# VectorE's filter arithmetic placed instruction by instruction between the steps of the ELU layer

## The chip, the cores and the metric

The kernel runs on one core of a Trainium2 chip. The metric is the device time of one execution in microseconds (us); lower is better. All data are float32.

## The reference

A global filter layer is followed by a two-layer network with an ELU. The filter is a real Fourier transform along the sequence, a product with a complex filter, and the inverse transform:

```python
X = np.fft.rfft(x, axis=1)              # x: 8 x 3008 x 256
F = (filt_r + 1j * filt_i)[None, :, :]  # 1505 x 256
y = np.fft.irfft(X * F, n=3008, axis=1)
t = y.reshape(24064, 256)
h = t @ w_in                            # 256 x 2048
g = np.where(h > 0.0, h, np.exp(np.minimum(h, 0.0)) - 1.0)
out = g @ w_out                         # 2048 x 256
```

## The kernel before

**Two kinds of work, interleaved.** There are eight images. The filter of image b is computed while the ELU layer of image b-1 runs; the first image's filter and the preparation of the weights come ahead of everything. The order of all instructions is written out by hand.

**The ELU layer.** An image has six token blocks (m = 0..5), each with four slices of the hidden layer (q = 0..3). One (b, m, q) is called a *quad*; 192 of them run one after the other, 24 (`PER`) for each image. Tokens come 512 at a time (448 for m = 0), as two halves. Both matrix products are done on 2 x 2 blocks with seven products instead of eight (Strassen's scheme in Winograd's form), so a quad has seven *up* steps (`up_steps`: into the hidden layer, matmuls on line 629) and seven *down* steps (`down_steps`: out of the hidden layer, matmuls on line 711; those of the quad before). A step is four matmuls. The loop at the end of the kernel deals the steps out by strings such as `"UUDUDDU"` and then `"DUUDUDD"`; quads in `opens` have other strings.

The seven products yield four blocks of the hidden layer: b11, b12, b21, b22. ScalarE copies single products out of PSUM (L640); VectorE adds the others to them (`add`, L637): b11 in up step `s2`, b22 in `s7`, b21 in `s4`. The bank `phd` is filled in `s7`, read by VectorE for b22, and then filled further in `s4`. The ELU takes two ScalarE instructions (`elu_exp`, L646 and L647) and one on VectorE (`elu_max`, L651, the maximum). By program order VectorE does in a quad: b11's add; the b22 add and the maximum of b11 (`s7`); the maximum of b12 (`s3`); b21's add and the maximum of b22 (`s4`); and in the tail two differences (L687, L688), the maximum of b21, and two more differences (L690, L691). In `s3`, ScalarE's exponentials of b12 and b22 are issued ahead of the maximum of b12.

After four quads the down products are combined: ScalarE copies two banks (L717), VectorE adds two of them and the two other banks in `tail` of `down_steps`, two more sums in `c_unit` a quad later, the last two and the transposes in `o_unit` the quad after that (all L728; transposes L753); then the output is written.

**Places.** `at(quad, place, fn, ...)` puts other work into a quad: place 2 after the third step of the first string and place 3 after its fifth, place 0 between the strings, place 1 behind the quad and its tails. This holds for one image's filter, with s the quad of its first step for a group g of frequencies (s = 6, 10, 14, 18 from the image's start):

- quad s, place 1: `b_unit`, the short transforms (TensorE), copies and sums;
- s + 1, place 2: `re_mult`, four products (L455, L456); place 1: `re_sums`, four sums (L462, L464);
- s + 2, place 2: three of the four products of `im_mult` (L472), all four for g = 4; place 1: the rest of them and `im_join`, two sums (L477);
- s + 3, place 2: `im_sums`, two sums (L482); place 1: `bi_unit`, the inverse short transforms, and the writes to DRAM.

`x_unit` (L230, L231) makes sums and differences of the inputs at place 0. `n_sums` (L604, L606) makes the five sums that the up steps need of a token block; for m = 1 two of them stand at place 2 of quad 2 of an image's 24, and three at place 1 of the same quad. The filter's table is read by GpSimd's DMA queue (`f_read`, L366), the intermediate tensors go through DRAM by SyncE's.

PSUM has four banks for the up steps and the transforms (`banks`, first in, first out) and four for the down steps.

Of the kernel before, what the change touches and what calls it, by code (L numbers as in the profile page):

```python
# [11 lines left out]
FP32 = mybir.dt.float32  # L12
U32 = mybir.dt.uint32
AXT = mybir.ActivationFunctionType
ALU = mybir.AluOpType
# [26 lines left out]
def _make_tables():  # L42
# [81 lines left out]
    tn = np.ascontiguousarray(tn.transpose(2, 1, 0, 3, 4, 5)).reshape(P, H, 64)  # L124
    once = np.stack([np.eye(P), gf.reshape(P, P)], 1)
    return [t.astype(np.float32) for t in (ta, tc, tn, np.stack([gb, gr, gi], 1), tf, once, pairs, tw)]


def order(m):
# [5 lines left out]
def kernel(  # L135
# [310 lines left out]
            nc.vector.tensor_tensor(out=t[:, k + 1], in0=t[:, k + 1], in1=ps, op=ALU.subtract)  # L446
        banks.extend(pf[p][0] for p in (0, 3, 1, 2))

    def re_mult(b, g):
        t, f = rs[b, g], fall[:, 0:2]  # L450
        z = ss[b, g] = qp.tile([P, 4, 2, D], FP32, tag="z", name="zs")
        if g == 0:
            nc.scalar.activation(out=t[0:32, :, 0, :], in_=once_in[0:32], func=AXT.Copy)
        for c in range(2):
            nc.vector.tensor_tensor(out=z[:, 2 + c], in0=t[:, c], in1=f[:, :, 0, c, :], op=ALU.mult)  # L455
            nc.vector.scalar_tensor_tensor(out=z[:, c], in0=t[:, 2 + c], scalar=-1.0, in1=f[:, :, 1, c, :],  # L456
                                           op0=ALU.mult, op1=ALU.mult)

    def re_sums(b, g):
        z = ss[b, g]  # L460
        for c in range(2):
            nc.vector.tensor_tensor(out=z[:, 2 + c], in0=z[:, 2 + c], in1=z[:, c], op=ALU.add)  # L462
        for c, op in ((0, ALU.add), (1, ALU.subtract)):
            nc.vector.tensor_tensor(out=z[:, c], in0=z[:, 2], in1=z[:, 3], op=op)  # L464
        if g == 0:
            nc.gpsimd.tensor_copy(out=z[0:32, 0:2, 0, :], in_=z[0:32, 2:4, 0, :])

    def im_mult(b, g, *parts):
        t, f = rs[b, g], fall[:, 0:2]
        for c, h in parts:  # L470
            k = 2 * h + c
            nc.vector.tensor_tensor(out=t[:, k], in0=t[:, k], in1=f[:, :, 1 - h, c, :], op=ALU.mult)  # L472

    def im_join(b, g):
        t = rs[b, g]
        for c in range(2):
            nc.vector.tensor_tensor(out=t[:, c], in0=t[:, c], in1=t[:, 2 + c], op=ALU.add)  # L477

    def im_sums(b, g):
        t, z = rs.pop((b, g)), ss[b, g]  # L480
        for c, op in ((0, ALU.subtract), (1, ALU.add)):
            nc.vector.tensor_tensor(out=z[:, 2 + c], in0=t[:, 0], in1=t[:, 1], op=op)  # L482
        if g == 0:
            for c in range(2):
                nc.gpsimd.tensor_copy(out=z[0:32, 2 + c, 0, :], in_=t[0:32, 1 - c, 0, :])

# [127 lines left out]
    def up_steps(b, m, q):  # L614

        h = half(m)
        y = ys[b, m]
        g = {}
        for tag, names in G_TAGS:
            t = gp.tile([P, len(names), 2, 256], FP32, tag=tag, name=tag)  # L620
            g.update({n: t[:, i, :, 0:h] for i, n in enumerate(names)})
        held = {}

        def mm(n, key, start):
            if start:
                held[key] = bank("ph" + key)
            ps = held[key][1]
            for a in range(2):
                nc.tensor.matmul(ps[:, a, 0:h], w_in[q][:, COMBO[n], a, :], y[n],  # L629
                                 start=start and a == 0, stop=True, skip_group_check=True)  # L630
            return ps[:, :, 0:h]

        def done(key):
            banks.append(held.pop(key)[0])

        def add(o, i0, i1):
            nc.vector.tensor_tensor(out=g[o], in0=i0, in1=i1, op=ALU.add)  # L637

        def keep(o, i0):
            nc.scalar.activation(out=g[o], in_=i0, func=AXT.Copy)  # L640

        es = {}

        def elu_exp(n, src):
            e = es[n] = ep.tile([P, 2, 256], FP32, tag="e", name="e")[:, :, 0:h]
            nc.scalar.activation(out=e, in_=src, func=AXT.Relu, scale=-1.0)  # L646
            nc.scalar.activation(out=e, in_=e, func=AXT.Exp, scale=-1.0)  # L647

        def elu_max(n, src):

            nc.vector.scalar_tensor_tensor(out=g[n], in0=es[n], scalar=1.0, in1=src, op0=ALU.subtract, op1=ALU.max)  # L651


        def s1():
            keep("t1", mm(1, "s", True))

        def s2():
            add("b11", mm(2, "a", True), g["t1"])
            done("a")

        def s6():
            keep("t2", mm(6, "s", False))

        def s5():
            keep("t4", mm(5, "s", False))

        def s7():
            elu_exp("b11", g["b11"])
            add("b22", mm(7, "d", True), g["t4"])
            elu_max("b11", g["b11"])  # L670

        def s3():
            p = mm(3, "s", False)
            elu_exp("b12", p)
            elu_exp("b22", g["b22"])
            elu_max("b12", p)
            done("s")

        def s4():
            add("b21", mm(4, "d", False), g["t2"])  # L680
            done("d")
            elu_max("b22", g["b22"])

        def tail():
            elu_exp("b21", g["b21"])
            t1, b12, b22 = g["t1"], g["b12"], g["b22"]
            nc.vector.tensor_tensor(out=t1, in0=b12, in1=g["b11"], op=ALU.subtract)  # L687
            nc.vector.tensor_tensor(out=b12, in0=b22, in1=b12, op=ALU.subtract)  # L688
            elu_max("b21", g["b21"])
            nc.vector.tensor_tensor(out=g["t2"], in0=b22, in1=t1, op=ALU.subtract)  # L690
            nc.vector.tensor_tensor(out=g["t4"], in0=g["b21"], in1=g["t2"], op=ALU.subtract)  # L691
            g_of[b, m, q] = {1: g["b11"], 2: g["b21"], 3: b22, 4: g["t4"], 5: t1, 6: g["t2"], 7: b12}

        return (s1, s2, s6, s5, s7, s3, s4), tail


    PLACE = {1: (0, 0), 5: (0, 1), 3: (1, 0), 7: (1, 1), 2: (2, 0), 6: (2, 1), 4: (3, 0)}

    def down_steps(b, m, q):
# [19 lines left out]
        def tail():  # L719
            if q != 3:  # L720
                return
            p1, p5 = (k[0][:, u, 0:h] for u in range(2))
            p35, p7 = (k[1][:, u, 0:h] for u in range(2))
            c = kp.tile([P, 2, 512], FP32, tag="c", name="c")
            (c11, c12), (c21, c22) = ((c[:, i, 0:h], c[:, i, h:2 * h]) for i in range(2))

            def add(o, i0, i1):
                nc.vector.tensor_tensor(out=o, in0=i0, in1=i1, op=ALU.add)  # L728

            add(p35, p35, p5)  # L730
            add(c12, po[2][:, 1, 0:h], p1)
            add(c11, po[2][:, 0, 0:h], p1)
            rest = [(p7, p7, c12), (c21, po[3][:, 0, 0:h], p7), (c12, c12, p35), (c22, p7, p5)]
            cs_[b, m] = c, lambda i: [add(*r) for r in rest[i:i + 2]]

        return [(lambda n=n: step(n)) for n in DOWNS], tail

# [2 lines left out]


    def c_unit(b, m):
        cs_[b, m][1](0)

    def o_unit(b, m):
        c, join = cs_.pop((b, m))
        join(2)
        o = kp.tile([P, 2, 2, 256], FP32, tag="k", name="o").rearrange("p i u (j s) -> p (i u j) s", s=64).rearrange("p j (e s) -> p j e s", e=2)
        if last(b, m):
            return o_last(b, m, c, o.rearrange("p (k f j) e s -> p k f (j e s)", k=2, f=2))  # L750
# [135 lines left out]
    with tc.manual_schedule():  # L886
# [135 lines left out]
        def at(quad, place, fn, *a):  # L1022
            plan.setdefault((quad, place), []).append((fn, a))
# [16 lines left out]
        for b in range(B):  # L1040
            t = (b - 1) * PER
            if b > 0:
# [15 lines left out]
                for g in range(0, NG, 2):  # L1058
# [4 lines left out]
                        if g:  # L1063
                            at(s - 1, 0, z_read, b, k)
                    at(s, 1, b_unit, b, g)
                    at(s + 1, 2, re_mult, b, g)
                    at(s + 1, 1, re_sums, b, g)
                    parts = ((0, 0), (0, 1), (1, 0), (1, 1))
                    early = 4 if g == 4 else 3
                    at(s + 2, 2, im_mult, b, g, *parts[:early])  # L1070
                    at(s + 2, 1, im_mult, b, g, *parts[early:])
                    at(s + 2, 1, im_join, b, g)
                    at(s + 3, 2, im_sums, b, g)
                    at(s + 3, 1, bi_unit, b, g)
                    at(s + 3, 1, y_write, b, g)
            for m, (s, sums) in enumerate(((23, (((23, 0), 0, 1, 2), ((24, 2), 3, 4))), (25, (((26, 2), 0, 1), ((26, 1), 2, 3, 4))),
                                           (25, (((29, 0), 0, 1), ((29, 1), 2, 3, 4))), (32, (((34, 2),),)),
                                           (32, (((38, 2),),)), (40, (((42, 2),),)))):
                if b == 0 and m == 1:
                    at(t + 23, 0, tn_read, b, m)  # L1080
                    at(t + 23, 0, y_read, b, m)
# [2 lines left out]
                elif b > 0 or m > 0:  # L1084
# [6 lines left out]
                    elif m in (1, 3):  # L1091
                        opens.add(t + s + 1)
                        at(t + s, 1, n_pair, b, m)
                    for (quad, place), *parts in sums:
                        at(t + quad, place, n_sums, b, m, *parts)
                if b == 0 and m == 1:
                    at(1, 1, w_join, 13)
# [4 lines left out]
        for i in range(-PER, len(items) + 3):  # L1102
# [9 lines left out]
                        fn(*a)  # L1112
            for fn, a in plan.get((i, 0), ()):
                fn(*a)
            for k in "DUUDUD" if i in opens else "DUUDUDD":
                s = ups if k == "U" else downs
                if s:
                    s.pop(0)()
            if up_tail:
                up_tail()  # L1120
            if down_tail:
# [35 lines left out]
```

## Time and profile before

| | us |
|---|---|
| three runs, median | 2557.44 |
| three runs, lowest and highest | 2554.37, 2557.8 |
| the profiled execution, its time | 2556.37 |
| the profiled execution, span from first to last instruction | 2554.6 |
| TensorE / VectorE / ScalarE / GpSimd busy | 2514.8 / 2116.5 / 1526.4 / 156.1 |

The granted TensorE clock is 0.996 of full speed in the mean; it is below full speed in start-up alone. An image's 24 quads take 308.7 us in the steady part. In the views below PE is TensorE's matmuls and PEld its weight loads, DVE is VectorE, ACT ScalarE, POOL GpSimd, SP SyncE; L is a line of the kernel. A row of the timeline gives the start, the time from the first start to the last end, the instruction, its output and inputs, the shape and how many instructions are merged; in brackets stands idle time ahead of it and what ended it. A row of the waits list gives the total, the number and the longest.

### The profile page before, as it was taken

The numbers are of one execution on the slowest core, as the hardware profiler recorded it, in microseconds if no ns is written. First come the engines' busy times: TensorE is split into PE (matmuls) and PEld (weight loads), VectorE is DVE, ScalarE is ACT, GpSimd is POOL, SyncE is SP. The second block draws the span as 40 slices with busy tenths as digits, with TensorE's granted clock in tenths as the row PEclk, the third lists the DMA queues.
The fourth block names the chain that finished last, engine by engine and source line by source line (L and its number), as shares of the span: only waits on it lengthen the run. The fifth ranks groups of instructions, "written<-read, shape, count | busy, mean of one in ns | idle before, by whom it ended". The sixth has DMA issues, their size and how long they took to land.

```text
span 2554.6 us, 45374 instructions
## 1 busy us (share of the span) xinstructions
PE 2514.8 (98%) x17266; PEld 2156.9 (84%) x17266; DVE 2116.5 (83%) x3649; ACT 1526.4 (60%) x2680; POOL 156.1 (6%) x315
## 2 busy tenths in 40 slices
PE   5999999999999999999999999999999999999999
PEld 4688889888898888988889888888888888898887
DVE  6978987888888888888888889788997889876666
ACT  6766556655565655565555655555555665565555
POOL 4000100010000100000000000000100001000000
PEclk8999999999999999999999999999999999999999
DMA  9662213523134232332224321343213322121010
GB/s 277 178 187 63 69 36 82 135 54 71 43 94 113 58 72 50 94 100 66 56 51 125 86 70 36 78 114 83 61 42 93 82 53 69 36 46 29 9 28 17
DMA packets 229454, 198.37 MB, mean 78 GB/s; under 512 B 128326, under 2 KB 201558, under 8 KB 229236
## 3 DMA queue, kind: packets, MB, share of 16 engines
q1 hardware_dynamic: 214740, 164.57, 26.2%
q0 software_dynamic: 14000, 30.44, 4.2%
q8 instruction: 136, 2.23, 0.4%
q14 instruction: 82, 0.67, 0.1%
q10 hardware_dynamic: 496, 0.46, 0.1%
HBM read 123.50 MB, written 78.12 MB: 79 GB/s over the span
## 4 chain that ended last, share of the span: by engine, by line
PE 93%; DVE 3%; DMA 2%; issue 1%; ACT 1%; POOL 0%; SPq 0%; DVEq 0%; POOLq 0%; ACTq 0%
PE po L711 43%; PE phs L629 24%; PE phd L629 12%; PE pha L629 6%; PE psn L578 2%; PE pf L427 1%; PE pv L499 1%; PE psa L246 1%; DVE g L637 1%; DMA fd<-in_filt_i_dram 1%; DVE g L651 0%; DMA t<-in_moe_w_out_dram 0%; DMA fd<-in_filt_r_dram 0%; DVE r L472 0%; PE po L372 0%
## 5 line engine op out<-in xcount | busy, mean ns | idle before, releaser
L711 PE MATMUL po<-g,wo 128*128 128x256 f32 (+1 forms) x5376 | 1318.6, 377 | 0.0
L711 PEld LDWEIGHTS po<-g,wo 128*128 128x128 f32 x5376 | 1012.0, 190 | 165.9 <-issue 52.3
L640 ACT ACTIVATE g<-phs 128x512 f32<-128x512 f32 (+1 forms) x576 | 338.6, 588 | 754.1 <-PE phs L629 753.5
L647 ACT ACTIVATE e<-e 128x512 f32<-128x512 f32 (+1 forms) x768 | 477.3, 621 | 24.3
L637 DVE TENSOR_TENSOR g<-phd,g 128x512 f32<-128x512 f32 (+1 forms) x384 | 259.3, 675 | 193.6 <-ACT e L647 129.3
L651 DVE SCALAR_TENSOR_TENSOR g<-e,g 128x512 f32<-128x512 f32 (+1 forms) x576 | 387.4, 673 | 8.5 <-ACT e L647 7.3
L629 PE MATMUL phs<-y,wi 128*128 128x256 f32 (+1 forms) x1536 | 387.6, 375 | 1.0 <-ACT y L553 1.0
L629 PE MATMUL phd<-y,wi 128*128 128x256 f32 (+1 forms) x1504 | 382.5, 377 | 1.3 <-DVE g L637 1.0
L646 ACT ACTIVATE e<-g 128x512 f32<-128x512 f32 (+1 forms) x576 | 354.5, 615 | 34.2 <-DVE g L637 24.0
L629 PEld LDWEIGHTS phs<-y,wi 128*128 128x128 f32 x1536 | 291.4, 190 | 34.4 <-ACT y L553 1.2
L629 PEld LDWEIGHTS phd<-y,wi 128*128 128x128 f32 x1504 | 283.3, 190 | 43.4 <-DVE g L637 11.9
L651 DVE SCALAR_TENSOR_TENSOR g<-e,phs 128x512 f32<-128x512 f32 (+1 forms) x192 | 129.8, 676 | 108.9 <-ACT e L647 108.9
L629 PE MATMUL phs<-yt,wi 128*128 128x256 f32 (+1 forms) x768 | 193.9, 375 | 0.9 <-ACT g L640 0.9
L629 PE MATMUL phs<-yb,wi 128*128 128x256 f32 (+1 forms) x768 | 193.8, 375 | 0.6 <-ACT g L640 0.6
L629 PE MATMUL pha<-yb,wi 128*128 128x256 f32 (+1 forms) x736 | 185.9, 375 | 0.0
L646 ACT ACTIVATE e<-phs 128x512 f32<-128x512 f32 (+1 forms) x192 | 112.2, 584 | 116.7 <-PE phs L629 116.6
L629 PEld LDWEIGHTS phs<-yt,wi 128*128 128x128 f32 x768 | 145.7, 190 | 17.9 <-ACT g L640 1.5
L629 PEld LDWEIGHTS phs<-yb,wi 128*128 128x128 f32 x768 | 143.4, 190 | 19.9 <-ACT g L640 1.0
L366 POOL DMA_DIRECT2D fall<-fp x224 | 110.0, 499 | 771.0 <-DVE r L472 745.2
L637 DVE TENSOR_TENSOR g<-pha,g 128x512 f32<-128x512 f32 (+1 forms) x192 | 129.3, 673 | 31.7 <-PE pha L629 31.7
L629 PEld LDWEIGHTS pha<-yb,wi 128*128 128x128 f32 x736 | 139.8, 190 | 16.1
L688 DVE TENSOR_TENSOR g<-g,g 128x512 f32<-128x512 f32 (+1 forms) x192 | 130.7, 681 | 6.6
(190 smaller groups left out, 2062.2 us busy)
## 6 DMA issues: line engine op xcount, KB each, us to landing
yd<-t SPq DMA_DIRECT2D x127, 192.0 KB
t<-yd SPq DMA_DIRECT2D x92, 256.0 KB
fall<-fp POOLq DMA_DIRECT2D x224, 96.0 KB, 2.9
t<-z SPq DMA_DIRECT2D x224, 96.0 KB
out_dram<-o SPq DMA_DIRECT2D x624, 32.0 KB
z<-t SPq DMA_DIRECT2D x144, 128.0 KB
xc<-in_x_dram SPq DMA_DIRECT2D x84, 128.0 KB
xc<-in_x_dram SPq DMA_DIRECT2D x161, 64.0 KB
```

What stands on the lines that cost most here:

```text
L246: nc.tensor.matmul(ps[k][1][a:a + 32, u, :], w[r, u, 32 * o:32 * o + 32], parts[o][r, u, :], start=True, stop=True, tile_position=(32 * k, a))
L366: nc.gpsimd.dma_start(t[32 * a:32 * a + 24].rearrange("p c u d -> p (c u d)"), fp[g, a].rearrange("q c u d -> q (c u d)"))
L427: nc.tensor.matmul(pf[p][1][32 * a:32 * a + 32, js, :], fb[r, v, :], t2[r, js, a, :], start=True, stop=True, tile_position=(32 * p, 32 * a))
L578: nc.tensor.matmul(o, t[r, i - 4 * m, ds(dh * P + 64 * c, 64)], w[r, i - 4 * m, :], start=True, stop=True)
L629: nc.tensor.matmul(ps[:, a, 0:h], w_in[q][:, COMBO[n], a, :], y[n], start=start and a == 0, stop=True, skip_group_check=True)
L637: nc.vector.tensor_tensor(out=g[o], in0=i0, in1=i1, op=ALU.add)
L640: nc.scalar.activation(out=g[o], in_=i0, func=AXT.Copy)
L646: nc.scalar.activation(out=e, in_=src, func=AXT.Relu, scale=-1.0)
L647: nc.scalar.activation(out=e, in_=e, func=AXT.Exp, scale=-1.0)
L651: nc.vector.scalar_tensor_tensor(out=g[n], in0=es[n], scalar=1.0, in1=src, op0=ALU.subtract, op1=ALU.max)
L688: nc.vector.tensor_tensor(out=b12, in0=b22, in1=b12, op=ALU.subtract)
L711: nc.tensor.matmul(po[i][:, u, 0:h], w_out[q][:, COMBO[n], a, :], g[n][:, a, :], start=q == 0 and a == 0 and n in (1, 3, 6, 4), stop=True, ...
```

## The change

The sixteen VectorE instructions of a filter group are numbered 0 to 15 and placed by a table, `FILTERED`, each with its quad after s and its place; one function `filtered` replaces the five functions. A new place 6 lies inside up step `s3`, behind ScalarE's exponentials of b12 and b22 and ahead of VectorE's maximum of b12. (Places 4 and 5 are added to the loop too, but no entry uses them.) Against the order before:

- sum 4, the first of the four of `re_sums`, goes from place 1 of quad s + 1 to its place 6;
- product 9, the third of `im_mult`, goes from place 2 of quad s + 2 to its place 6;
- product 11 stands at place 1 of quad s + 2 for every group; for g = 4 it stood at place 2;
- the table `SUMS` does the same for `n_sums`; only m = 1 changes, whose third sum goes from place 1 of quad 2 to its place 6;
- the down join `p35 += p5` goes from the `tail` of `down_steps` to `o_unit`, two quads later, ahead of the join that reads it.

The arithmetic is the same, and so is the number of instructions.

```diff
+FILTERED = (((1, 2), (0, 2, 1, 3)), ((1, 6), (4,)), ((1, 1), (5, 6, 7)), ((2, 2), (8, 10)), ((2, 6), (9,)),
+            ((2, 1), (11, 12, 13)), ((3, 2), (14, 15)))
+SUMS = ((((23, 0), (0, 1, 2)), ((24, 2), (3, 4))), (((26, 2), (0, 1)), ((26, 6), (2,)), ((26, 1), (3, 4))),
+        (((29, 0), (0, 1)), ((29, 1), (2, 3, 4))), (((34, 2), (0, 1, 2, 3, 4)),), (((38, 2), (0, 1, 2, 3, 4)),),
+        (((42, 2), (0, 1, 2, 3, 4)),))
...
-    def re_mult(b, g):
+    def filtered(b, g, *parts):
+
         t, f = rs[b, g], fall[:, 0:2]
...
+        for i in parts:
+            c, k, h = i % 2, i % 4 // 2, i // 4
+            if h == 0:
+                if k == 0:
+                    nc.vector.tensor_tensor(out=z[:, 2 + c], in0=t[:, c], in1=f[:, :, 0, c, :], op=ALU.mult)
+                else:
+                    nc.vector.scalar_tensor_tensor(out=z[:, c], in0=t[:, 2 + c], scalar=-1.0, in1=f[:, :, 1, c, :],
+                                                   op0=ALU.mult, op1=ALU.mult)
+            elif h == 1:
+                if k == 0:
+                    nc.vector.tensor_tensor(out=z[:, 2 + c], in0=z[:, 2 + c], in1=z[:, c], op=ALU.add)
+                else:
+                    nc.vector.tensor_tensor(out=z[:, c], in0=z[:, 2], in1=z[:, 3], op=(ALU.add, ALU.subtract)[c])
+            elif h == 2:
+                nc.vector.tensor_tensor(out=t[:, 2 * k + c], in0=t[:, 2 * k + c], in1=f[:, :, 1 - k, c, :], op=ALU.mult)
+            elif k == 0:
+                nc.vector.tensor_tensor(out=t[:, c], in0=t[:, c], in1=t[:, 2 + c], op=ALU.add)
+            else:
+                nc.vector.tensor_tensor(out=z[:, 2 + c], in0=t[:, 0], in1=t[:, 1], op=(ALU.subtract, ALU.add)[c])
...
@@ up step s3
             elu_exp("b12", p)
             elu_exp("b22", g["b22"])
+            for fn, a in plan.get(((b * 6 + m) * 4 + q, 6), ()):
+                fn(*a)
             elu_max("b12", p)
...
@@ tail of down_steps
-            add(p35, p35, p5)
             add(c12, po[2][:, 1, 0:h], p1)
             add(c11, po[2][:, 0, 0:h], p1)
-            rest = [(p7, p7, c12), (c21, po[3][:, 0, 0:h], p7), (c12, c12, p35), (c22, p7, p5)]
-            cs_[b, m] = c, lambda i: [add(*r) for r in rest[i:i + 2]]
+            rest = [(p7, p7, c12), (c21, po[3][:, 0, 0:h], p7), (p35, p35, p5), (c12, c12, p35), (c22, p7, p5)]
+            cs_[b, m] = c, lambda *parts: [add(*rest[i]) for i in parts]
...
-        cs_[b, m][1](0)
+        cs_[b, m][1](0, 1)
...
-        join(2)
+        join(2, 3, 4)
...
-                    at(s + 1, 2, re_mult, b, g)
-                    at(s + 1, 1, re_sums, b, g)
-                    parts = ((0, 0), (0, 1), (1, 0), (1, 1))
-                    early = 4 if g == 4 else 3
-                    at(s + 2, 2, im_mult, b, g, *parts[:early])
-                    at(s + 2, 1, im_mult, b, g, *parts[early:])
-                    at(s + 2, 1, im_join, b, g)
-                    at(s + 3, 2, im_sums, b, g)
+                    for (quad, place), parts in FILTERED:
+                        at(s + quad, place, filtered, b, g, *parts)
```

More of the change, by code (lines that the diff above doesn't have):

```diff
@@ L447, in b_unit @@
         banks.extend(pf[p][0] for p in (0, 3, 1, 2))
-    def re_mult(b, g):
+    def filtered(b, g, *parts):
         t, f = rs[b, g], fall[:, 0:2]
[L451 to L457, printed above, removed]
@@ L459, in re_sums @@
-    def re_sums(b, g):
-        z = ss[b, g]
[L461 to L465, printed above, removed]
-            nc.gpsimd.tensor_copy(out=z[0:32, 0:2, 0, :], in_=z[0:32, 2:4, 0, :])
[L468 to L483, printed above, removed]
+        if 0 in parts:
+            ss[b, g] = qp.tile([P, 4, 2, D], FP32, tag="z", name="zs")
+            if g == 0:
+                nc.scalar.activation(out=t[0:32, :, 0, :], in_=once_in[0:32], func=AXT.Copy)
@@ L484, in im_sums @@
+        if g == 0 and 7 in parts:
+            nc.gpsimd.tensor_copy(out=z[0:32, 0:2, 0, :], in_=z[0:32, 2:4, 0, :])
+        if g == 0 and 15 in parts:
             for c in range(2):
@@ L1065 @@
                     at(s, 1, b_unit, b, g)
-                    at(s + 1, 2, re_mult, b, g)
-                    at(s + 1, 1, re_sums, b, g)
-                    parts = ((0, 0), (0, 1), (1, 0), (1, 1))
-                    early = 4 if g == 4 else 3
-                    at(s + 2, 2, im_mult, b, g, *parts[:early])
-                    at(s + 2, 1, im_mult, b, g, *parts[early:])
-                    at(s + 2, 1, im_join, b, g)
-                    at(s + 3, 2, im_sums, b, g)
+                    for (quad, place), parts in FILTERED:
+                        at(s + quad, place, filtered, b, g, *parts)
                     at(s + 3, 1, bi_unit, b, g)
                     at(s + 3, 1, y_write, b, g)
-            for m, (s, sums) in enumerate(((23, (((23, 0), 0, 1, 2), ((24, 2), 3, 4))), (25, (((26, 2), 0, 1), ((26, 1), 2, 3, 4))),
-                                           (25, (((29, 0), 0, 1), ((29, 1), 2, 3, 4))), (32, (((34, 2),),)),
-                                           (32, (((38, 2),),)), (40, (((42, 2),),)))):
+            for m, s in enumerate((23, 25, 25, 32, 32, 40)):
+                sums = SUMS[m]
                 if b == 0 and m == 1:
@@ L1093 @@
                         at(t + s, 1, n_pair, b, m)
-                    for (quad, place), *parts in sums:
+                    for (quad, place), parts in sums:
                         at(t + quad, place, n_sums, b, m, *parts)
@@ L1114 @@
                 fn(*a)
-            for k in "DUUDUD" if i in opens else "DUUDUDD":
+            for n, k in enumerate("DUUDUD" if i in opens else "DUUDUDD"):
                 s = ups if k == "U" else downs
@@ L1118 @@
                     s.pop(0)()
+                if n in (2, 4):
+                    for fn, a in plan.get((i, 4 + n // 4), ()):
+                        fn(*a)
             if up_tail:
```

## The prediction

> **What bounds the kernel now.** The page comes first: the busy times and the chain that ended last.
>
> ```profile
> PE 2514.8 (98%) x17266; PEld 2156.9 (84%) x17266; DVE 2116.5 (83%) x3649; ACT 1526.4 (60%) x2680; POOL 156.1 (6%) x315
> ...
> PE 93%; DVE 3%; DMA 2%; issue 1%; ACT 1%; POOL 0%; SPq 0%; DVEq 0%; POOLq 0%; ACTq 0%
> PE po L711 43%; PE phs L629 24%; PE phd L629 12%; PE pha L629 6%; PE psn L578 2%; PE pf L427 1%; PE pv L499 1%; PE psa L246 1%; DVE g L637 1%; DMA fd<-in_filt_i_dram 1%; DVE g L651 0%; DMA t<-in_moe_w_out_dram 0%; DMA fd<-in_filt_r_dram 0%; DVE r L472 0%; PE po L372 0%
> ...
> ```
>
> TensorE is the bound and its matmuls are the same before and after. A change in VectorE's order can only win or lose TensorE's waits. So the second view is the list of waits of the weight loads, from 160 to 2215 us (after start-up, before the last image's stretch):
>
> ```profile
> PEld phd L629 <- DVE g L637: 11.6, 27, 0.5
> ```
>
> The fourth step's matmuls add into the PSUM bank `phd`, which VectorE must first have read for block b22 (L637). 27 times it hasn't. That list shows nothing else of VectorE's that matters. By their times these waits repeat every 24 quads: in quad 3, 8, 12 and 20 of a period (I number quads so, from each image's start). Quads 8, 12, 20 come seven times, quad 3 six times.
>
> The timeline of one quad 12 shows how such a wait is built:
>
> ```profile
> 1177.98 1.03 PE L629 MATMUL phd<-y,wi 128*128 128x256 f32 x4
> 1178.17 1.88 DVE L472 TENSOR_TENSOR r<-r,fall 128x512 f32<-128x512 f32 x3
> 1178.85 1.03 PE L629 MATMUL phs<-y,wi 128*128 128x256 f32 x4
> 1179.44 0.63 ACT L647 ACTIVATE e<-e 128x512 f32<-128x512 f32 x1
> 1179.49 0.84 PEld L711 LDWEIGHTS po<-g,wo 128*128 128x128 f32 x4
> 1179.71 1.03 PE L711 MATMUL po<-g,wo 128*128 128x256 f32 x4
> 1179.97 0.68 DVE L637 TENSOR_TENSOR g<-phd,g 128x512 f32<-128x512 f32 x1
> 1180.57 0.68 DVE L651 SCALAR_TENSOR_TENSOR g<-e,g 128x512 f32<-128x512 f32 x1
> 1180.59 0.63 ACT L647 ACTIVATE e<-e 128x512 f32<-128x512 f32 x1
> 1180.71 1.13 PE L629 MATMUL phd<-y,wi 128*128 128x256 f32 x4
> 1180.71 0.73 PEld L629 LDWEIGHTS phd<-y,wi 128*128 128x128 f32 x4 [0.38 <-DVE g L637]
> 1181.25 0.69 DVE L651 SCALAR_TENSOR_TENSOR g<-e,phs 128x512 f32<-128x512 f32 x1
> 1181.68 1.89 PE L711 MATMUL po<-g,wo 128*128 128x256 f32 x8
> 1181.88 0.69 DVE L637 TENSOR_TENSOR g<-phd,g 128x512 f32<-128x512 f32 x1
> ```
>
> Undisturbed groups of four matmuls start 0.865 us apart (1177.98, 1178.85, 1179.71). The next two should start at 1180.57 and 1181.44; the second starts at 1181.68. So the wait costs 0.24: 0.14 until VectorE's add for b22 has ended (1179.97 + 0.68 = 1180.65, then 0.06), and 0.10 because the first weight load isn't hidden (the group takes 1.13, not 1.03). Normally a load starts one matmul, 0.22, ahead of its own matmul (1179.49 against 1179.71). A b22 that ends 0.22 + 0.06, say 0.27, before its matmul is due costs nothing; call that the need.
>
> **The stalls that the change reaches.** The same reading, from one down group to the next, in quads 8, 20 and 3:
>
> ```profile
> 1125.96 1.03 PE L711 MATMUL po<-g,wo 128*128 128x256 f32 x4
> ...
> 1128.01 1.24 PE L711 MATMUL po<-g,wo 128*128 128x256 f32 x5
> ...
> 1283.24 1.03 PE L711 MATMUL po<-g,wo 128*128 128x256 f32 x4
> ...
> 1285.21 0.59 PE L711 MATMUL po<-g,wo 128*128 128x256 f32 x2
> ...
> 1060.27 0.92 PE L629 MATMUL phs<-y,wi 128*128 128x224 f32 x4
> 1061.03 0.92 PE L711 MATMUL po<-g,wo 128*128 128x224 f32 x4
> ...
> 1062.97 1.11 PE L711 MATMUL po<-g,wo 128*128 128x224 f32 x5
> ```
>
> Two groups should take 1.73, and 1.51 to 1.52 at quad 3's width of 224 (0.76 a group). They take 2.05, 1.97 and 1.94: losses of 0.32, 0.24 and 0.42. Seven times 0.32 + 0.24 + 0.24 and six times 0.42 are 5.6 + 2.5 = 8.1 us, all that can be won here.
>
> **Filter products and sums (quads 7 to 21).** L472's three products stand between b11's add and b22's add in quads 8, 12 and 20, 0.60 us each (1.88 is two steps of 0.60 and one duration of 0.68). After the change two stand there; the third goes behind the maximum of b11. One L464/L462 step that ran ahead of the quad moves into the quad before. VectorE thus reaches b22 up to 1.2 us sooner. It can't start b22 before its first matmuls have ended, but 0.24 to 0.32 plus the 0.22 of the load is all that is needed. I credit the whole loss, 5.6.
>
> What pays for it is the maximum of b12. In quad 12 the maximum of b11 can start once its exponential ends (1179.44 + 0.63 = 1180.07), at 1180.12 instead of 1180.57. The placed product takes the next step of 0.60, to 1180.72, and the maximum of b12 then starts at 1181.32. Its own exponential ends at 1181.22, so it could not have started before 1181.27; today it is at 1181.25. It is late by 0.07, and the tail behind it by no more. In quads 7, 11, 15 and 19 the placed sum falls into real idle time:
>
> ```profile
> 1116.23 0.69 DVE L651 SCALAR_TENSOR_TENSOR g<-e,phs 128x512 f32<-128x512 f32 x1 [0.79 <-ACT e L647]
> ```
>
> 0.79 idle holds one step of 0.60 (the row is quad 7's). ScalarE's order is unchanged; DMA issues keep their places behind the quad. The filter reads that POOL issues in quad 16 wait for L472's last product, which moves behind the quad's tail there; what they load is first used in quad 19, tens of us later.
>
> **Next to become late** are the quads behind: 13 and 21, and 17, where VectorE has no idle time before b22.
>
> ```profile
> 1191.87 0.68 DVE L637 TENSOR_TENSOR g<-phd,g 128x512 f32<-128x512 f32 x1
> ...
> 1192.90 1.03 PE L629 MATMUL phd<-y,wi 128*128 128x256 f32 x4
> ...
> 1243.94 0.68 DVE L637 TENSOR_TENSOR g<-phd,g 128x512 f32<-128x512 f32 x1
> ...
> 1245.18 1.03 PE L629 MATMUL phd<-y,wi 128*128 128x256 f32 x4
> ```
>
> Quad 13's b22 ends 0.35 before its matmul. TensorE comes 0.24 sooner, but the tail in front loses one join (0.34, next part): 0.45, less the need 0.18 to spare. Quad 17's ends 0.56 before; behind quad 16's tail there is one product more (+0.60, since the special case of four early products goes) and one join less (-0.34): 0.30, or 0.03 to spare. Both hold, the second narrowly; both ends of that are in the rivals.
>
> **The second-layer input sums (quad 2).** One L604 sum leaves the row of work ahead of quad 3:
>
> ```profile
> 1056.58 0.62 DVE L691 TENSOR_TENSOR g<-g,g 128x448 f32<-128x448 f32 x1
> 1057.12 0.42 DVE L604 TENSOR_TENSOR yt<-y,y 128x256 f32<-128x256 f32 x1
> 1057.57 0.42 DVE L604 TENSOR_TENSOR y<-yt,yb 128x256 f32<-128x256 f32 x1
> 1057.91 0.42 DVE L604 TENSOR_TENSOR y<-yb,yt 128x256 f32<-128x256 f32 x1
> ...
> 1061.44 0.62 DVE L637 TENSOR_TENSOR g<-phd,g 128x448 f32<-128x448 f32 x1
> ```
>
> From here to b22 VectorE has no gap, so b22 moves by the step that goes: 0.45 (a sum whose result the next one reads; 0.34 without that). It ends at 1060.99 + 0.62 = 1061.61, and the load can start at 1061.67. The load is due one matmul (0.19) before 1061.03 + 0.76 = 1061.79, at 1061.60. It is still 0.07 late, so I credit 0.35 of the 0.42: 2.1 instead of 2.5.
>
> **The join `p35 += p5`** goes from the down tail to `o_unit`, two quads later. Nothing new reads it early. In `o_unit` it stands ahead of the join that reads its result, so it costs 0.45 there, once in four quads, before b22. That is spare everywhere but in one place: the image without filter work has a stall of its own.
>
> ```profile
> 2379.81 1.03 PE L711 MATMUL po<-g,wo 128*128 128x256 f32 x4
> ...
> 2381.74 0.59 PE L711 MATMUL po<-g,wo 128*128 128x256 f32 x2
> ```
>
> 1.93 instead of 1.73: `o_unit` stands ahead of this b22, and the loss grows by 0.45. At the very end the join now lies on the path; today it runs while the last matmuls do.
>
> ```profile
> 2546.17 0.43 DVE L728 TENSOR_TENSOR k<-k 128x256 f32<-128x256 f32 x1 [1.10 <-ACT k L717]
> ...
> 2549.14 0.42 DVE L728 TENSOR_TENSOR c<-k 128x256 f32<-128x256 f32 x1
> ```
>
> Everything behind comes 0.45 later.
>
> **Sum:** 5.6 + 2.1 - 0.45 - 0.45 = 6.8 us won. The profiled execution took 2556.37 (span 2554.6), so 2549.6; the median of the three runs is 1.07 higher, which gives 2550.6. I put the forecast between them, at 2550.1.
>
> **Rivals.** *The placed instruction is paid in full (slower).* VectorE runs in order, so whatever the placed product adds to the maximum of b12 goes through b21 and the tail to the next quad's b22. With X us added, quads 13 and 21 stall by X - 0.18 and quad 17 by X - 0.03. From X = 0.46 these three (2X - 0.36 + X - 0.03 = 0.99, times seven) eat the 6.8. For it: today the maximum of b12 follows that of b11 in quad 12 without a gap. Against it: that is so because b11's own maximum is late there; both wait for exponentials whose times the rows give, and X comes out at 0.07. At X = 0.75 (the whole instruction and the lateness) the sum is 13.0 lost, 6.8 won: 2562.6 from the profiled run, 2563.7 from the median. Chance 0.06.
>
> *Steps are longer than they look.* If one VectorE instruction could start only when the one before has ended, 0.68 apart, X in quad 12 would be 1180.12 + 0.68 + 0.68 = 1181.48 less 1181.25, 0.23. Quads 13 and 21 would lose 0.05 each and quad 17 0.20: seven times 0.30 is 2.1, leaving 4.7 won: 2552.2. The rows speak against it, as L472's three take 1.88 and not 2.04, and L637 to L651 at 1179.97 and 1180.57 are 0.60 apart. The Trainium skill, page "VectorE: DVE Perf Modes", section "The DRAIN you can't avoid", says that the next instruction does not start until the pipe of the one before is empty; by that rule this rival would hold, and the trace agrees only as far as the starts lie 0.60 apart. Chance 0.07.
>
> *The won time is met by another wait.* TensorE arrives sooner at the filter's and the inputs' matmuls, or quad 17 loses its spare 0.03 and the 0.10 of a bare load with it. If half is lost, 3.4 remain: 2553.0 from the profiled run, 2554.0 from the median. For it: several starts of VectorE are within 0.1 of their limits. Against: the waits list has no such line today. Chance 0.11.
>
> *Nothing reaches the end:* 2556.4 to 2557.4, chance 0.03. The forecast keeps 0.73.
>
> **The numbers.** A change under 0.2%, 5.1 us, can't be told from none here: the three runs themselves spread over 3.4 us. Faster by more than that takes the forecast alone, less 0.03 for a measurement that falls short of 5.1: 0.70. Within 0.2%: that 0.03, the two middle rivals and most of the last: 0.23. Slower: the first rival and 0.01 of the last: 0.07. The range runs from the lowest run less all that could be won, 2554.37 - 8.1 = 2546.3, to the half-lost case from the median, 2554.0, rounded up to 2554.3 for the unknown of 0.3 in quad 17.
>
> **What would show it.** Right: the waits list of the weight loads has 7 or fewer rows of `phd` on L637 where there were 27, down groups in quads 8, 12 and 20 lie 1.73 apart, in quad 3 at most 1.60; the maximum of b12 in quad 12 starts within 0.1 of its exponential's end, with one L472 between the two maxima; the last `c<-k` comes 0.45 later after the last matmul. Wrong: `phd` waits in quads 13, 17 or 21, a VectorE gap between the placed product and the maximum, or the same 27 waits.

## The result and the profile after

The changed kernel takes 2547.24 us (median of 20 runs, 2544.51 to 2555.47), the kernel before 2554.43 (median of 20 runs). The ratio is 0.9973, with a 95% interval of 0.9966 to 0.9979: 0.27% or about 7 us faster. The forecast was 2550.1 in a range of 2546.3 to 2554.3, and 6.8 us won.

The page of the changed kernel, busy times and the chain that ended last (its lines have other numbers: L715 are the down matmuls, L631 the up matmuls, L639 the adds of the blocks, L653 the maxima, L649 the second ScalarE instruction of an ELU, L474 and L476 the sums 4 to 7, L478 the products 8 to 11, L606 the sums of the token blocks, L732 the down joins):

```profile
span 2544.9 us, 45370 instructions
PE 2507.5 (99%) x17266; PEld 2158.4 (85%) x17266; DVE 2119.8 (83%) x3649; ACT 1524.0 (60%) x2680; POOL 156.9 (6%) x315
...
PE 96%; DMA 2%; DVE 1%; ACT 1%; issue 0%; SPq 0%; ACTq 0%; DVEq 0%
...
```

VectorE has as many instructions as before, and its share of the chain went from 3% to 1%. The list of waits of the weight loads, 160 to 2215 us, no longer has the line `phd ... <- DVE` with its 27 waits. These are its first row (`issue`: the profile shows nothing that was waited for) and the only one in which VectorE still appears, at the input transforms, as it did before:

```profile
PEld po L715 <- issue: 50.4, 73, 0.8
...
PEld psa L253 <- DVE g L639: 1.0, 6, 0.2
```

To see where the time went, I take the start of up step `s2` (the first `pha` matmul of a quad) in both traces and subtract quad by quad. In the six periods from the second on, the mean differences are -0.43 in quad 3, -0.35 in quad 8, -0.24 in quad 12, -0.25 in quad 20, and at most 0.01 in the other twenty: 1.26 us a period. The first period has -0.34, -0.24 and -0.25, without quad 3. In the last image quad 10 is 0.46 longer, and from the last quad's `s2` to the end it is 0.75. The sum is -7.21. (The two executions also differ by 2.49 us ahead of the first quad, where nothing was changed; that is left out here and below.)

Quad 12 in the timeline, as in the prediction:

```profile
1170.91 1.28 DVE L478 TENSOR_TENSOR r<-r,fall 128x512 f32<-128x512 f32 x2
...
1172.46 0.69 DVE L639 TENSOR_TENSOR g<-phd,g 128x512 f32<-128x512 f32 x1 [0.26 <-PE phd L631]
1172.78 0.63 ACT L649 ACTIVATE e<-e 128x512 f32<-128x512 f32 x1
1173.05 1.03 PE L715 MATMUL po<-g,wo 128*128 128x256 f32 x4
...
1173.44 0.69 DVE L653 SCALAR_TENSOR_TENSOR g<-e,g 128x512 f32<-128x512 f32 x1 [0.30 <-ACT e L649]
1173.91 1.03 PE L631 MATMUL phd<-y,wi 128*128 128x256 f32 x4
1173.93 0.63 ACT L649 ACTIVATE e<-e 128x512 f32<-128x512 f32 x1
1174.05 0.69 DVE L478 TENSOR_TENSOR r<-r,fall 128x512 f32<-128x512 f32 x1
...
1174.65 0.68 DVE L653 SCALAR_TENSOR_TENSOR g<-e,phs 128x512 f32<-128x512 f32 x1
1174.78 1.46 PE L715 MATMUL po<-g,wo 128*128 128x256 f32 x6
...
1175.25 0.69 DVE L639 TENSOR_TENSOR g<-phd,g 128x512 f32<-128x512 f32 x1
```

Two products instead of three stand ahead of b22 (L639 at 1172.46), and VectorE now waits for TensorE there, 0.26, and not the other way round. b22 ends at 1173.15, 0.76 before its matmul at 1173.91. Down groups are 1.73 apart (1173.05, 1174.78) where they were 1.97. The maximum of b11 waits 0.30 for its exponential; the placed product (1174.05) comes 0.61 later and the maximum of b12 0.60 after that, at 1174.65. Its exponential ended at 1173.93 + 0.63 = 1174.56, so the product holds it up by a few hundredths.

Quad 3, behind the token block's sums:

```profile
1051.25 0.42 DVE L606 TENSOR_TENSOR y<-yt,yb 128x256 f32<-128x256 f32 x1
1051.59 0.42 DVE L606 TENSOR_TENSOR y<-yb,yt 128x256 f32<-128x256 f32 x1
...
1055.11 0.62 DVE L639 TENSOR_TENSOR g<-phd,g 128x448 f32<-128x448 f32 x1
1055.16 0.92 PE L715 MATMUL po<-g,wo 128*128 128x224 f32 x4
...
1055.78 0.70 PEld L631 LDWEIGHTS phd<-y,wi 128*128 128x128 f32 x4
1055.91 0.92 PE L631 MATMUL phd<-y,wi 128*128 128x224 f32 x4
...
1056.67 0.54 PE L715 MATMUL po<-g,wo 128*128 128x224 f32 x2
```

Two sums instead of three; b22 ends at 1055.73, 0.18 before its matmul, and the down groups are 1.51 apart, the undisturbed distance.

### The profile page after: what moved, and what is told of

Read it like the earlier page. It is cut to its first block, busy times and chain, and to the rows that moved or that the text cites. A ratio compares the mean times of both kernels' runs of the same rounds, so it can differ in the third digit from the quotient of the medians.

```text
span 2544.9 us, 45370 instructions
## 1 busy us (share of the span) xinstructions
PE 2507.5 (99%) x17266; PEld 2158.4 (85%) x17266; DVE 2119.8 (83%) x3649; ACT 1524.0 (60%) x2680; POOL 156.9 (6%) x315
## 4 chain that ended last, share of the span: by engine, by line
PE 96%; DMA 2%; DVE 1%; ACT 1%; issue 0%; SPq 0%; ACTq 0%; DVEq 0%
PE po L715 45%; PE phs L631 25%; PE phd L631 13%; PE pha L631 6%; PE psn L580 2%; PE pf L434 1%; PE pv L501 1%; DMA xc<-in_x_dram 1%; PE psa L253 1%; PE po L379 1%; DMA x<-in_x_dram 0%; PE po L334 0%; PE psr L379 0%; PE psa L272 0%; DVE g L639 0%
## 5 line engine op out<-in xcount | busy, mean ns | idle before, releaser
L715 PE MATMUL po<-g,wo 128*128 128x256 f32 (+1 forms) x5376 | 1318.5, 377 | 0.0
L715 PEld LDWEIGHTS po<-g,wo 128*128 128x128 f32 x5376 | 1011.9, 190 | 166.0 <-issue 52.4
L642 ACT ACTIVATE g<-phs 128x512 f32<-128x512 f32 (+1 forms) x576 | 338.7, 588 | 749.4 <-PE phs L631 749.2
L649 ACT ACTIVATE e<-e 128x512 f32<-128x512 f32 (+1 forms) x768 | 477.4, 622 | 24.4
L639 DVE TENSOR_TENSOR g<-phd,g 128x512 f32<-128x512 f32 (+1 forms) x384 | 259.4, 676 | 194.4 <-ACT e L649 115.7
L653 DVE SCALAR_TENSOR_TENSOR g<-e,g 128x512 f32<-128x512 f32 (+1 forms) x576 | 387.8, 673 | 14.5 <-ACT e L649 14.4
L631 PE MATMUL phs<-y,wi 128*128 128x256 f32 (+1 forms) x1536 | 387.5, 375 | 0.4 <-ACT y L555 0.4
L631 PE MATMUL phd<-y,wi 128*128 128x256 f32 (+1 forms) x1504 | 379.7, 375 | 0.4 <-DVE g L639 0.4
L631 PEld LDWEIGHTS phs<-y,wi 128*128 128x128 f32 x1536 | 291.4, 190 | 33.9 <-ACT y L555 0.6
L631 PEld LDWEIGHTS phd<-y,wi 128*128 128x128 f32 x1504 | 285.2, 190 | 33.7 <-DVE g L639 0.8
L653 DVE SCALAR_TENSOR_TENSOR g<-e,phs 128x512 f32<-128x512 f32 (+1 forms) x192 | 129.8, 676 | 88.4 <-ACT e L649 88.4
L631 PE MATMUL phs<-yt,wi 128*128 128x256 f32 (+1 forms) x768 | 193.9, 375 | 0.9 <-ACT g L642 0.9
L631 PE MATMUL phs<-yb,wi 128*128 128x256 f32 (+1 forms) x768 | 193.8, 375 | 0.6 <-ACT g L642 0.6
L631 PE MATMUL pha<-yb,wi 128*128 128x256 f32 (+1 forms) x736 | 185.9, 375 | 0.0
L631 PEld LDWEIGHTS phs<-yt,wi 128*128 128x128 f32 x768 | 145.7, 190 | 18.0 <-ACT g L642 1.5
L631 PEld LDWEIGHTS phs<-yb,wi 128*128 128x128 f32 x768 | 143.4, 190 | 19.9 <-ACT g L642 1.0
L639 DVE TENSOR_TENSOR g<-pha,g 128x512 f32<-128x512 f32 (+1 forms) x192 | 129.4, 674 | 32.8 <-PE pha L631 32.7
L631 PEld LDWEIGHTS pha<-yb,wi 128*128 128x128 f32 x736 | 139.8, 190 | 16.1
```

The source lines that it names most:

```text
L715: nc.tensor.matmul(po[i][:, u, 0:h], w_out[q][:, COMBO[n], a, :], g[n][:, a, :], start=q == 0 and a == 0 and n in (1, 3, 6, 4), stop=True, ...
```

## The experiments

Each run's quads are compared as above, with the traces of the kernel before and of the changed kernel. Such differences mostly repeat within 0.02 us from period to period, though single quads are off by up to 0.12, so a quad's figure is its mean over the six periods; whole runs spread over several us, so causes are read from the quads and the runs' medians stand beside them.

**Filter table alone.** From the changed kernel: the join back in the tail, the old sums.

```diff
-SUMS = ... (((26, 2), (0, 1)), ((26, 6), (2,)), ((26, 1), (3, 4))),
+SUMS = ... (((26, 2), (0, 1)), ((26, 1), (2, 3, 4))),
...
@@ tail of down_steps
+            add(p35, p35, p5)
...
-        join(2, 3, 4)
+        join(2, 3)
```

> Filter table alone (sums of quad 2 and the join p35 as before). Theory A (a stall of b22's matmul goes when b22's add ends about 0.16 us before it; slack in the next quads decides the rest): against the kernel before, quads 8, 12 and 20 take 0.35, 0.24 and 0.25 us less, quad 3 the same, quads 13 and 21 0 to 0.1 more (spare falls from 0.54 to 0.20), quad 17 0.26 more, since the join stands ahead of its b22 again and the spare of 0.24 turns into -0.10; start-up aside 4 us less in all. Theory B (any VectorE work taken from in front of b22 is won, nothing is lost behind): 5.9 us less, quad 17 unchanged. Theory C (the join's move made the gain): no change in quads 8, 12, 20.

Measured: quads 8, 12 and 20 -0.34, -0.24 and -0.25; quad 17 +0.25; quads 3, 13 and 21 within 0.01 (0.07 in a single quad 13); 4.03 us less in all. The median is 2550.91 against 2554.39 (ratio 0.9987, interval 0.9978 to 0.9996). Theory A holds: the filter's three stalls go, and one new stall of 0.25 comes in quad 17. B and C fall.

**The token block's sum alone**, filter and join as before.

> The third sum of the m = 1 token block alone moved into place 6 of quad 2. Theory A: quad 3 takes 0.43 us less in six periods, 2.6 us in all, nothing else moves. Rival (the stall of quad 3 is the input sums' own, and moves with them): quad 3 unchanged or only partly less, up to 0.35.

Measured: quad 3 -0.43 in each of the six periods, all other quads within 0.01 (one quad 8 of the first period -0.07); 2.57 us less, without the very first quad. That one is 0.41 longer here, because this execution's granted clock is still 0.5 until 91.8 us, 1.1 us into that quad. Median 2552.01, ratio 0.9988 (0.9978 to 0.9997). The whole stall goes, as theory A had it.

**The join alone**, filter and sums as before.

> The join p35 alone moved to o_unit. Theory A: the periods take the same time as before (27 waits stay); quad 10 of the last image takes 0.42 to 0.46 us more and the end behind the last matmul 0.46 more: about 0.9 us slower, below what the runs can tell. Rival (the join's move helps by itself): quads 8, 12 or 20 get shorter, since the tails ahead are shorter.

Measured: no quad of the periods changes by more than 0.01, and the 27 waits are there again. Quad 10 of the last image +0.46, the end +0.73: 1.2 us slower by the trace, median 2554.81, ratio 1.0005 (0.9996 to 1.0015). By itself the join's move only costs.

**The changed kernel with the join back in the tail.**

```diff
+            add(p35, p35, p5)
             add(c12, po[2][:, 1, 0:h], p1)
...
-        join(2, 3, 4)
+        join(2, 3)
```

> The changed kernel with the join p35 back in the tail. Theory A: against the changed kernel 0.9 us are won at the last image and the end, but quad 17's b22 ends 0.10 after its matmul is due and loses 0.26 seven times, 1.8 us; quads 13 and 21 fall to a spare of 0.20 and lose 0 to 0.1. So 1 to 2 us slower than the changed kernel, 5 to 6 faster than before. Rival (the join's move is pure loss): 0.9 faster than the changed kernel, quads 13, 17 and 21 unchanged.

Measured: quad 17 +0.26 against the changed kernel, quads 13 and 21 within 0.01 (0.07 in a single quad 13), and the 1.2 us at the last image and the end won back: 6.55 less than before, 0.66 more than the changed kernel. Median 2547.02, ratio 0.9969 (0.9957 to 0.9981), which can't tell it from the changed kernel; the quads can. Quad 17 of this kernel in the timeline:

```profile
1238.70 1.03 PE L715 MATMUL po<-g,wo 128*128 128x256 f32 x4
1238.99 0.68 DVE L639 TENSOR_TENSOR g<-phd,g 128x512 f32<-128x512 f32 x1
...
1239.72 0.73 PEld L631 LDWEIGHTS phd<-y,wi 128*128 128x128 f32 x4 [0.39 <-DVE g L639]
1239.72 1.13 PE L631 MATMUL phd<-y,wi 128*128 128x256 f32 x4
...
1240.69 1.67 PE L715 MATMUL po<-g,wo 128*128 128x256 f32 x7
```

The old picture in a new quad: b22 ends at 1239.67, 0.10 after the matmul was due (1238.70 + 0.865), and the down groups are 1.99 apart. In the changed kernel the same b22 ends in time:

```profile
1237.35 0.68 DVE L639 TENSOR_TENSOR g<-phd,g 128x512 f32<-128x512 f32 x1
1237.40 1.03 PE L715 MATMUL po<-g,wo 128*128 128x256 f32 x4
...
1238.27 1.03 PE L631 MATMUL phd<-y,wi 128*128 128x256 f32 x4
```

It has 0.24 in hand and loses nothing. So the join's move is a guard: it takes 0.34 out of the tail ahead of quad 17.

**The join late, but not for the last image**, where no filter runs. This is the version that the first four runs point to.

```diff
+            if b == B - 1:
+                add(p35, p35, p5)
             add(c12, po[2][:, 1, 0:h], p1)
...
-        join(2, 3, 4)
+        join(*(2, 3, 4)[b == B - 1:])
```

> The changed kernel with the join p35 back in the tail for the last image alone, where no filter runs. Theory A (the join's move only guards quad 17 and costs 0.46 in quad 10 of the last image and about 0.74 at the end): these 1.2 us are won, everything else as in the changed kernel: 8.4 us less than before, start-up aside. Rival (the end is set by the output transfers): 0.46 won, the end unchanged.

Measured: every quad as in the changed kernel within 0.03 but two: quad 10 of the last image -0.45 and the end -0.76. In all 8.4 us less than before. Median 2546.10, ratio 0.9966 (0.9953 to 0.9978). By the trace it beats the changed kernel by 1.2 us; the runs can't separate the two. The end of this kernel and of the changed one:

```profile
2538.29 0.76 DVE L732 TENSOR_TENSOR c<-po,k 128x256 f32<-128x256 f32 x2 [0.67 <-PE po L715]
...
2541.22 0.69 DVE L780 COPY o<-pso 128x512 f32<-128x512 f32 x1 [0.64 <-PE pso L778]
```

```profile
2536.88 0.76 DVE L732 TENSOR_TENSOR c<-po,k 128x256 f32<-128x256 f32 x2 [2.27 <-PE po L715]
...
2538.42 0.42 DVE L732 TENSOR_TENSOR k<-k 128x256 f32<-128x256 f32 x1
...
2540.27 0.69 DVE L778 COPY o<-pso 128x512 f32<-128x512 f32 x1 [0.64 <-PE pso L776]
```

From the first join to the last copy it is 2.93 without the late join (`k<-k` at 2538.42) and 3.39 with it, 0.46 more. Of the remaining 0.3, some 0.22 lie after that copy: 3.69 to the end of the span here (2545.6 less 2541.91), 3.92 there (2544.88 less 2540.96). The other 0.07 lie ahead of the first join: it starts 0.45 before the last down matmul without the late join and 0.38 with it. Both came in every kernel with the late join at the end and in none without; what makes them stays open.

**Product 9 behind the quad**, not in the activation.

```diff
-FILTERED = ... ((2, 2), (8, 10)), ((2, 6), (9,)),
-            ((2, 1), (11, 12, 13)), ((3, 2), (14, 15)))
+FILTERED = ... ((2, 2), (8, 10)),
+            ((2, 1), (9, 11, 12, 13)), ((3, 2), (14, 15)))
```

> The changed kernel, but product 9 goes behind the quad (place 1) and not into the activation. Theory A (a quad loses 0.155 less the time by which its b22 ends before its matmul is due): quads 8, 12, 20 as in the changed kernel; the tail in front of quads 13, 17, 21 is 0.5 to 0.6 us longer, so quads 13 and 21 lose 0.12 to 0.21 each and quad 17 0.42 to 0.51: 4.6 to 6.5 us slower than the changed kernel. Theory B (it only matters that the product leaves the front of b22): same as the changed kernel.

Measured against the changed kernel: quads 13 and 21 +0.16, quad 17 +0.46, the rest within 0.02: 5.5 us slower. Median 2552.99, ratio to the kernel before 0.9991 (0.9981 to 1.0). The waits list, 160 to 2250 us, has 21 waits again:

```profile
PEld phd L631 <- DVE g L639: 8.2, 21, 0.6
```

They are in other quads than before. It isn't enough that work leaves the front of b22: behind the quad it stands in front of the next b22. Inside the activation it stands where VectorE would wait.

**Sum 4 alone in the activation**, product 9 ahead of b22 as before.

```diff
-FILTERED = ... ((2, 2), (8, 10)), ((2, 6), (9,)),
+FILTERED = ... ((2, 2), (8, 10, 9)),
             ((2, 1), (11, 12, 13)), ((3, 2), (14, 15)))
```

> The changed kernel, but product 9 stays ahead of b22 (place 2); only sum 4 of the filter is inside the activation. Theory A: one step fewer ahead of b22 is enough, it ends 0.3 to 0.45 before its matmul is due in quads 8, 12 and 20: no quad differs from the changed kernel by over 0.03. Rival (both instructions are needed): the waits of quads 8, 12 and 20 come back in part, 0.1 us or more each, 2 us in all.

Measured: no quad differs from the changed kernel by more than 0.01 in the mean. Median 2546.32, ratio 0.9969 (0.9958 to 0.9980). Moving product 9 isn't needed for the time; one step fewer ahead of b22 suffices.

**Both behind the maximum of b12** instead of in front of it.

```diff
-FILTERED = ... ((1, 6), (4,)), ... ((2, 6), (9,)),
+FILTERED = ... ((1, 4), (4,)), ... ((2, 4), (9,)),
```

> The changed kernel, but sum 4 and product 9 stand right behind the maximum of b12 (after step s3) and not in front of it. Theory A (in front of the maximum VectorE would wait for the exponential anyway; behind it the instruction pushes b21 and the tail): quads 8, 12, 20 as in the changed kernel; b21 0.47 to 0.53 later, quads 13 and 21 lose 0.08 to 0.15 each and quad 17 0.38 to 0.45: 3.9 to 5.2 us slower than the changed kernel. Rival (VectorE has room there too): same as the changed kernel.

Measured against the changed kernel: quads 13 and 21 +0.16 and quad 17 +0.46, but also quad 8 +0.20 and quads 12, 16 and 20 +0.17: 10.3 us slower (without the very first quad, 0.36 longer with the granted clock at 0.5 until 91.3 us), twice what theory A had, and slower than before: median 2558.61 against 2554.98, ratio 1.0013 (1.0004 to 1.0022). The direction was right; the price missed a path. The waits list, 160 to 2250 us, shows it:

```profile
PEld phs L631 <- ACT g L642: 8.5, 28, 0.3
PEld phd L631 <- DVE g L639: 8.2, 21, 0.6
```

28 waits are for ScalarE's copy of the first product, a wait that the same list of the kernel before doesn't have. The timeline from quad 7 into quad 8:

```profile
1116.66 0.69 DVE L653 SCALAR_TENSOR_TENSOR g<-e,phs 128x512 f32<-128x512 f32 x1 [0.79 <-ACT e L649]
1117.27 0.68 DVE L474 TENSOR_TENSOR zs<-zs 128x512 f32<-128x512 f32 x1
1117.87 0.69 DVE L639 TENSOR_TENSOR g<-phd,g 128x512 f32<-128x512 f32 x1
...
1118.59 0.63 ACT L648 ACTIVATE e<-g 128x512 f32<-128x512 f32 x1 [0.78 <-DVE g L639]
1119.25 0.63 ACT L649 ACTIVATE e<-e 128x512 f32<-128x512 f32 x1
1119.49 1.03 PE L715 MATMUL po<-g,wo 128*128 128x256 f32 x4
1119.79 0.58 ACT L642 ACTIVATE g<-phs 128x512 f32<-128x512 f32 x1
...
1120.42 1.13 PE L631 MATMUL phs<-yt,wi 128*128 128x256 f32 x4
```

The sum behind the maximum pushes b21 (L639), b21 pushes its two ScalarE instructions, and these stand ahead of the next quad's copy out of `phs` (L642). It ends at 1120.37, the third up step starts at 1120.42, 0.07 late and with a bare weight load (1.13). In the changed kernel the sum is in front of the maximum, and VectorE still waits 0.20 for the exponential behind it:

```profile
1109.05 0.68 DVE L474 TENSOR_TENSOR zs<-zs 128x512 f32<-128x512 f32 x1
...
1109.93 0.69 DVE L653 SCALAR_TENSOR_TENSOR g<-e,phs 128x512 f32<-128x512 f32 x1 [0.20 <-ACT e L649]
...
1110.53 0.68 DVE L639 TENSOR_TENSOR g<-phd,g 128x512 f32<-128x512 f32 x1
1111.25 0.63 ACT L648 ACTIVATE e<-g 128x512 f32<-128x512 f32 x1 [0.18 <-DVE g L639]
...
1112.45 0.58 ACT L642 ACTIVATE g<-phs 128x512 f32<-128x512 f32 x1
1112.75 1.03 PE L715 MATMUL po<-g,wo 128*128 128x256 f32 x4
1113.61 1.03 PE L631 MATMUL phs<-yt,wi 128*128 128x256 f32 x4
```

There the copy ends at 1113.03, 0.58 before its matmul, and b21 starts 2.22 before the down group (1110.53, 1112.75); behind the maximum the sum leaves 1.62 (1117.87, 1119.49). Its whole step of 0.60 is paid.

## Why the prediction was right

**The bound and the 27 stalls** were read rightly: nothing but these stalls, one quad and the end changed, and the quads are those named.

**The filter's term** was 5.6; the quads give 0.83 in the first period and 0.84 in each of six, 5.9. Its share of the change, with its own cost in quad 17, is what the first experiment shows.

**Quad 3's term** was sized too small: 2.1 against six times 0.43, 2.6. The step that failed is the need of 0.27, the time by which b22 must end ahead of its matmul. I took the whole lead of a normal weight load. Call the time by which b22 ends before its matmul is due the time in hand. In the changed kernel quad 3 has 0.18 and quad 17 0.24, and neither loses; with product 9 behind the quad, quads 13 and 21 have nothing in hand and lose 0.16; quad 17 with the join in the tail has -0.10 and loses 0.26; the stalls of before have -0.08 or worse. A loss of 0.155 less the time in hand fits all of these. Between 0 and 0.18 the six periods have only the two single quads 13 that lost 0.07, in the first and the fourth experiment. This is the latter:

```profile
878.67 1.03 PE L715 MATMUL po<-g,wo 128*128 128x256 f32 x4
878.77 0.68 DVE L639 TENSOR_TENSOR g<-phd,g 128x512 f32<-128x512 f32 x1
...
879.50 0.73 PEld L631 LDWEIGHTS phd<-y,wi 128*128 128x128 f32 x4 [0.21 <-DVE g L639]
879.53 1.10 PE L631 MATMUL phd<-y,wi 128*128 128x256 f32 x4
...
880.47 1.89 PE L715 MATMUL po<-g,wo 128*128 128x256 f32 x8
```

b22 ends at 879.45, 0.08 before its matmul is due (878.67 + 0.865). The matmul starts on time, but its load is only 0.03 ahead of it, and the down groups are 1.80 apart: 0.07 lost, as the formula has it. In quad 3 the load is 0.13 ahead (1055.78 against 1055.91) and nothing is lost. So of the load's 0.22 lead only about 0.10 is needed, and 0.05 for the wait to end.

The same number explains why quad 17 held. The prediction gave it 0.30 in hand and quad 13 0.45; the changed kernel has 0.24 and 0.54. By the need of 0.27 quad 17 would have lost. It lost nothing because it has 0.08 above 0.155: the forecast came true, but not for the reason given.

**The join's cost** was 0.45 and 0.45. The first is 0.46. The second is 0.75, of which 0.46 are the instruction that I counted; no term stood for the other 0.3.

**The sum:** 5.9 + 2.6 - 0.46 - 0.75 = 7.3, by the quads 7.21, predicted 6.8; the errors lie in opposite directions, and that they partly cancel is luck. The absolute forecast was 2.9 too high, because it hung on three runs with a median of 2557.44; over 20 runs the kernel before has 2554.43, and 6.8 less is 2547.6. So the measured 2547.24 lies only 0.9 above the low end of the range.

**The rivals.** The instruction paid in full did not happen, since the maximum waits for its exponential anyway; but product 9 behind the quad and both instructions behind the maximum show what such a push costs: 5.5 and 10.3 us. The push that I priced went through VectorE alone; the path through ScalarE's order to the copy out of `phs` was missing in it. Longer steps did not happen either: at 1173.44, 1174.05 and 1174.65 three VectorE instructions of 0.69, 0.69 and 0.68 start 0.61 and 0.60 apart, each about 0.08 before the recorded end of the one ahead. The Trainium skill (page "VectorE: DVE Perf Modes", section "The DRAIN you can't avoid") adds to the rule that the prediction took from it that an instruction that is not held starts earlier. These rows agree with the addition, and the rival rested on the rule without it. No wait took the place of those that went.

**What wasn't seen ahead:** that one of the two placed instructions is enough. The prediction moved both and credited the sum of them; its own rows would have told that one step of 0.60 covers the 0.17 by which b22 was late in quad 8 (0.32 less 0.155) and even the 0.27 that it held necessary.

## What to carry to other kernels

When one engine is the bound and its work is fixed, list its waits with their places and price the change by those alone; then follow each moved instruction to the next wait of the same kind, one unit of work later. On an engine that runs in order, the place for extra work is in front of an instruction that waits for another engine, as far as that wait is long enough; one instruction further on, the sum cost its whole step of 0.60 here, on its own engine and then on the one that reads the results. Price a late operand from the time at which the load of the weights needs it, and measure that lead rather than assume the whole of it.

## What the runs showed of the hardware

A matmul group whose first weight load has to wait past the due time loses 0.10 us on top of the wait (it takes 1.13 instead of 1.03 in quad 17 with the join in the tail), as the next group starts that much later. A load that starts 0.06 us later than usual costs nothing (quad 3: 0.13 ahead of its matmul, against a lead of 0.19 at that width); one that starts 0.03 ahead instead of 0.22 costs 0.07 (the single quad 13). And whole executions of one kernel spread over 6 to 11 us (20 runs each of the kernel before and the changed one), while the duration of one quad mostly repeats within 0.02 us between executions, with single quads off by up to 0.12.
